# Three small edits to a fused retention and feed-forward kernel: the order of one down product, the slots of one block's attention steps, and the store of the last output

## The chip, the cores and the metric

One core of a Trainium2 chip. The metric is device time in microseconds (us), the median of several executions; ratios come with a 95% interval. A trace is one profiled execution of a kernel, timed from the start of its span.

## The reference, cut to what matters

```python
scores = scale * q @ k^T                      # 8 batches, 8 heads, 576 positions, 64 wide
ret = scores * (gamma_h ** (i - j) if i >= j else 0)
x = (ret @ v) regrouped to (4608 tokens, 512)
h = x @ w_in                                  # 512 -> 2048
g = h * clip(h + 3, 0, 6) / 6
out = g @ w_out                               # 2048 -> 512, float32
```

## The kernel before

The attention is done in chunks of 128 positions with a running state per head (each batch has four chunks of 128 and a rest of 64; they are numbered through all batches). The feed-forward part is done in token blocks: number 0 has 512 tokens, 1 to 3 are small, 4 to 10 have 512 each. I count blocks from 0, so "the first block" is number 0 and "the fourth block" is number 4. Pieces ("subs") of the feed-forward work, each worth one slot of about 0.87 us of TensorE (PE), are interleaved with attention steps by a list of slots that is written by hand. Each engine's own instructions stand in its queue in that order.

One attention step `i` asks every engine for something:

```python
    def step(i):
        stage(inter, i - 1)          # PE: state part of chunk i-1
        if chunks_at(i) < NCH:
            stage(update, i)         # PE: new state sum
            stage(keep, i)           # VectorE: state;  GpSimd: sd = state * decay
        stage(score, i)              # PE: scores;  VectorE: masked scores "at" (two)
        stage(mix, i - 1)            # PE: at @ v;  ScalarE: xt
        stage(cast, i + 3)           # GpSimd: three casts or products of loaded tiles
        if i + 3 > NCH + NPE - 1:
            stage(xpose, i + 3)      # SyncE: DMA transpose of q and k
        stage(load, i + 6)           # SyncE: loads
```

The first block's down product takes each 128-token row chunk `mc` through four quarters (`part`) of the second weight, which arrives by four DMAs, one per quarter:

```python
    def down(kb, mc, part):
        # ...
        for fc in range(m * part, m * part + m):
            nc.tensor.matmul(pout, gts[kb][:, fc, P * mc:P * mc + P],
                             wout16[:, fc, :],
                             start=(fc == 0), stop=(fc == NFC - 1))
        # part 3: copy to osb by ScalarE, give the PSUM bank back, store every second mc
```

From the fourth block on, the down product is a scheme of seven half-size products (`seven`), for each half `u` of the block, which needs four sums of activation quarters made by VectorE (`gsums`; eight instructions a block, two fp16 inputs from SBUF each):

```python
    def gsums(kb, i):
        # ...
        for u in range(2):
            nc.vector.tensor_tensor(out=s[i][:, :, u], in0=x[:, :, u],
                                    in1=y[:, :, u], op=op)
```

Order of a block: 16 up products (each followed by `u` on ScalarE and `gt` on VectorE), gsums 0 and 1, products 1 and 2 for both `u`, gsums 2 and 3, products 5 and 6, then 7, then 4 and 3. A block half's output is a tile `osb` of 128 x 2 x 512 floats, stored by one 512 KB DMA after product 3.

## Time and profile before

312.0 us (311.6 to 312.81, three runs). The page of the profiled run:

```profile
span 309.8 us, 6856 instructions
PE 295.2 (95%) x2644; PEld 190.1 (61%) x2644; DVE 234.5 (76%) x435; ACT 162.8 (53%) x307; POOL 125.8 (41%) x154
```

PE (TensorE) is busy for 295.2 us. What can be won without doing fewer matmuls is in the gaps. I cut the span by the starts of PE's first matmul of each stage in the timeline (the span is 309.77 us before the page rounds it):

| stretch of PE's time | us, before |
|---|---|
| start to the first block's first down matmul | 33.87 |
| from there to the second block's first up matmul | 17.94 |
| from there to the fourth block's first up matmul | 40.23 |
| from there to the next block's first up matmul | 35.24 |
| from there to the end of the last matmul | 178.35 |
| from there to the end of the span | 4.14 |

Here is PE's timeline in the first block's down product: start, duration, engine, line, output<-inputs, shapes, count, and in brackets the idle time just before and what ended it.

```profile
41.00 1.03 PE L529 MATMUL pout<-wout,gt 128*128 128x512 f16 x4
41.96 0.26 PE L327 MATMUL pm<-qkt 64*64 64x64 f16 x8
43.65 1.89 PE L529 MATMUL pout<-wout,gt 128*128 128x512 f16 x8 [1.43 <-DMA wout<-in_moe_w_out_dram]
```

Row chunk 0 has its quarter 2 at 41.00 and at once wants quarter 3, which lands 1.43 us too late.

The fourth block's seven products, on PE, VectorE (DVE) and GpSimd (POOL):

```profile
114.02 1.04 PE L594 MATMUL accz<-wt,gsum 128*128 128x256 f16 x8
116.91 1.05 PE L594 MATMUL accy<-wt,gsum 128*128 128x256 f16 x8 [1.85 <-DVE gsum L574]
120.83 1.05 PE L594 MATMUL accy<-wt,gsum 128*128 128x256 f16 x8 [0.25 <-DVE gsum L574]
...
110.82 0.85 DVE L305 TENSOR_TENSOR state<-pu,sd 64x256 f16<-64x256 f32 x2
111.70 1.29 DVE L333 TENSOR_TENSOR at<-pm,cmask 128x512 f16<-128x512 f32 x2
112.91 2.50 DVE L574 TENSOR_TENSOR gsum<-gt 128x1024 f16<-128x1024 f16 x2
115.33 2.54 DVE L574 TENSOR_TENSOR gsum<-gsum,gt 128x1024 f16<-128x1024 f16 x2
...
113.37 1.49 POOL L111 TENSOR_TENSOR natqk<-stgqk,wvq 128x512 f16<-128x512 f32 x1
114.82 1.49 POOL L114 TENSOR_TENSOR natv<-stgv,wvq 128x512 f16<-128x512 f32 x1
```

Two things delay the gsum that PE waits for. The step in slot 16 put 2.1 us of VectorE work (state and masked scores, 110.82 to 112.91) ahead of the gsums; and a pair of gsums takes 2.50 us here while GpSimd works beside them, and 1.29 in every later block, where it does not. GpSimd's products are slow at the same moment: 1.49 us against 1.04 elsewhere.

The end of the run:

```profile
304.59 1.04 PE L594 MATMUL accz<-wout,gsum 128*128 128x256 f16 x8
305.67 0.42 DVE L613 TENSOR_TENSOR osb<-accz,csum 128x256 f32<-128x256 f32 x1 [1.32 <-PE accz L594]
```

The last store (512 KB) is issued at 306.2, its bytes move until 308.3, and the span ends at 309.8. One of its windows of half a microsecond (start:end, length, busy time of PE, PEld, DVE, ACT, POOL with counts, granted clock, share of the 16 DMA engines, GB/s):

```profile
307.00:307.50 0.50, 0.00 (x0) 0.00 (x0) 0.00 (x0) 0.00 (x0) 0.00 (x0) 1.00 1.03 426
```

### The profile page before, as it was taken

Reading aid. Unit: us, or ns where it says so; the run is one execution under the profiler, and the core shown is the slowest. Engines: PE = TensorE matmul, PEld = TensorE weight load, DVE = VectorE, ACT = ScalarE, POOL = GpSimd, SP = SyncE. Lnnn points to the kernel's source line nnn. Section 1 sums busy time; section 2 is a strip of 40 time slices with the busy share of each in tenths; the row PEclk is TensorE's granted clock in tenths of the full one; section 3 lists DMA queues with packets and bytes.
Section 4 is the critical chain, followed back from the end, with each engine's and each line's share of the span. In section 5 each row is a group of like instructions: output and inputs, shape, how many; then the busy total and the mean of one; then the engine's idle time right before and its main releaser. Section 6 shows DMA issues by size and latency. Waiting matters only on the chain.

```text
span 309.8 us, 6856 instructions
## 1 busy us (share of the span) xinstructions
PE 295.2 (95%) x2644; PEld 190.1 (61%) x2644; DVE 234.5 (76%) x435; ACT 162.8 (53%) x307; POOL 125.8 (41%) x154
## 2 busy tenths in 40 slices
PE   7799989989999988999999999999999999999994
PEld 3454436677655467646864686468646864684583
DVE  6697447565948999699778977897789778856781
ACT  7567325565437732575357534753575347526721
POOL 3681139664576759052192409131754130000000
PEclk9999999999999999999999999999999999999998
DMA  7999999999799799999068965791694040003003
GB/s 247 204 194 196 196 193 209 238 240 220 174 202 246 177 220 235 187 252 203 9 155 234 215 146 135 223 236 40 187 245 111 2 156 0 2 0 138 1 0 138
DMA packets 143217, 49.61 MB, mean 160 GB/s; under 512 B 134224, under 2 KB 140368, under 8 KB 143184
## 3 DMA queue, kind: packets, MB, share of 16 engines
q1 hardware_dynamic: 138960, 44.97, 62.8%
q0 software_dynamic: 4224, 4.19, 8.2%
q8 instruction: 21, 0.34, 0.4%
q14 instruction: 12, 0.10, 0.1%
HBM read 36.70 MB, written 9.44 MB: 149 GB/s over the span
## 4 chain that ended last, share of the span: by engine, by line
PE 76%; DMA 10%; DVE 5%; POOL 3%; ACT 3%; issue 1%; SPq 0%; DVEq 0%
PE ph L512 35%; PE accy L594 15%; DMA wout<-in_moe_w_out_dram 7%; PE accz L594 7%; PE pout L529 6%; PE po L354 4%; PE accx L594 3%; PE pm L323 3%; DMA stgk<-in_k_dram 2%; DVE gsum L574 2%; PE po L252 2%; PE pu L274 2%; ACT u L516 1%; POOL natv L465 1%; DVE at L333 1%
## 5 line engine op out<-in xcount | busy, mean ns | idle before, releaser
L512 PE MATMUL ph<-xt,win 128*128 128x512 f16 (+2 forms) x704 | 130.1, 341 | 0.8 <-ACT xt L387 0.7
L517 DVE SCALAR_TENSOR_TENSOR gt<-u,ph 128x512 f16<-128x512 f32 x144 | 96.2, 686 | 29.4 <-ACT u L516 28.3
L516 ACT ACTIVATE u<-ph,cb 128x512 f32<-128x512 f32 x144 | 99.1, 688 | 35.1 <-PE ph L512 32.8
L512 PEld LDWEIGHTS <-win 128*128 128x128 f16 x704 | 61.6, 98 | 59.3 <-DMA win<-in_moe_w_in_dram 1.5
L310 POOL TENSOR_TENSOR sd<-state,gp 128x512 f32<-128x512 f16 x21 | 22.8, 1088 | 99.5 <-DVE state L305 62.1
L594 PEld LDWEIGHTS <-gsum 128*128 128x128 f16 x448 | 43.6, 98 | 7.8 <-DVE gsum L574 2.7
L604 ACT COPY csum<-accy 128x256 f32<-128x256 f32 x42 | 15.6, 373 | 46.3 <-PE accy L594 46.3
L387 ACT ACTIVATE xt<-po 128x512 f16<-128x512 f32 (+2 forms) x57 | 23.2, 438 | 30.2 <-PE po L354 29.8
L333 DVE TENSOR_TENSOR at<-pm,cmask 128x512 f16<-128x512 f32 x56 | 36.1, 687 | 0.9
L594 PEld LDWEIGHTS <-gt 128*128 128x128 f16 x336 | 31.8, 98 | 6.4 <-DVE gt L517 0.4
L111 POOL TENSOR_TENSOR natqk<-stgqk,wvq 128x512 f16<-128x512 f32 x28 | 30.5, 1091 | 6.0 <-DMA stgqk<-in_q_dram 6.0
L114 POOL TENSOR_TENSOR natv<-stgv,wvq 128x512 f16<-128x512 f32 x28 | 30.6, 1091 | 5.5 <-DMA stgv<-in_v_dram 5.5
L529 PE MATMUL pout<-wout,gt 128*128 128x512 f16 x128 | 30.7, 380 | 1.4 <-DMA wout<-in_moe_w_out_dram 1.4
L594 PE MATMUL accy<-wt,gsum 128*128 128x256 f16 x224 | 26.9, 273 | 2.1 <-DVE gsum L574 2.1
L110 POOL CAST natqk<-stgqk 128x512 f16<-128x512 f32 (+1 forms) x36 | 23.2, 645 | 6.0 <-PE ph L512 6.0
L305 DVE TENSOR_TENSOR state<-pu,sd 64x256 f16<-64x256 f32 x42 | 17.6, 420 | 5.4 <-PE pu L274 4.5
L574 DVE TENSOR_TENSOR gsum<-gt 128x1024 f16<-128x1024 f16 x28 | 20.3, 765 | 0.2
L529 PEld LDWEIGHTS <-gt 128*128 128x128 f16 x128 | 11.4, 98 | 13.7 <-issue 1.4
L354 PE MATMUL po<-at,natv 128*64 128x128 f16 (+1 forms) x320 | 15.8, 220 | 0.8 <-DVE at L333 0.7
L594 PE MATMUL accx<-wout,gt 128*128 128x256 f16 x112 | 14.9, 273 | 0.0
L594 PE MATMUL accy<-wt,gt 128*128 128x256 f16 x112 | 14.6, 273 | 0.0
L594 PE MATMUL accy<-wout,gt 128*128 128x256 f16 x112 | 14.5, 273 | 0.0
(75 smaller groups left out, 245.4 us busy)
## 6 DMA issues: line engine op xcount, KB each, us to landing
out_dram<-osb SPq DMA_DIRECT2D x17, 512.0 KB, 4.3
stgv<-in_v_dram SPq DMA_DIRECT2D x32, 256.0 KB, 4.3
stgqk<-in_k_dram SPq DMA_DIRECT2D x28, 256.0 KB, 3.7
stgqk<-in_q_dram SPq DMA_DIRECT2D x28, 256.0 KB, 4.0
win<-in_moe_w_in_dram POOLq DMA_DIRECT2D x4, 512.0 KB, 10.2
wout<-in_moe_w_out_dram POOLq DMA_DIRECT2D x4, 512.0 KB, 19.0
stgq<-in_q_dram SPq DMA_DIRECT2D x2, 512.0 KB, 5.3
stgk<-in_k_dram SPq DMA_DIRECT2D x2, 512.0 KB, 6.1
```

The costliest lines, as they stand in the source:

```text
L110: nc.gpsimd.tensor_copy(n16[:, 0], t[:, 0])
L111: nc.gpsimd.tensor_tensor(out=n16[:, 1], in0=t[:, 1], in1=w[:, 1].unsqueeze(2).to_broadcast(sh), op=ALU.mult)
L114: nc.gpsimd.tensor_tensor(out=v16, in0=tv, in1=w[:, 0].unsqueeze(2).to_broadcast(sh), op=ALU.mult)
L333: nc.vector.tensor_tensor(out=at, in0=pms[e], in1=w[:, e], op=ALU.mult)
L354: nc.tensor.matmul(o_ap, v_ap, a_ap, start=(c == 0 and pr == 0), stop=True, skip_group_check=True)
L387: nc.scalar.mul(x, src, inv_sqrt_d)
L512: nc.tensor.matmul(ph[:, j, :], win16[:, dmc, P * fc:P * fc + P], xts[kb][:, dmc, :], start=(dmc == 0), stop=(dmc == NCC - 1))
L516: nc.scalar.activation(u, ph, ACTF.Relu, bias=cb[:, 0:1], scale=1.0 / 6.0)
L517: nc.vector.scalar_tensor_tensor(out=gts[kb][:, g * m:g * m + m, :], in0=u, scalar=1.0, in1=ph, op0=ALU.min, op1=ALU.mult)
L529: nc.tensor.matmul(pout, gts[kb][:, fc, P * mc:P * mc + P], wout16[:, fc, :], start=(fc == 0), stop=(fc == NFC - 1))
L574: nc.vector.tensor_tensor(out=s[i][:, :, u], in0=x[:, :, u], in1=y[:, :, u], op=op)
L594: nc.tensor.matmul(o, a[:, f, u, :], w[:, f, :], start=(first and f == 0), stop=(f == HF - 1), skip_group_check=True)
```

## The change

Intent: (1) use all four row chunks' quarter-2 matmuls to cover the arrival of quarter 3; (2) move the attention steps of the fourth block so that they stay clear of its gsums; (3) leave only a quarter of the last tile to be stored after the last addition.

```diff
@@ seven(): the last block's second half
         elif p == 4:
             nc.scalar.copy(osb[:, 1, 0:HD], o)
             done_with(t)
+            if tok0 + 256 * u + 256 == NTOK:
+                o2 = out[NTOK - 256:NTOK, :].rearrange("(p h) n -> p h n", h=2)
+                nc.sync.dma_start(o2[:, 0, 0:HD], osb[:, 0, 0:HD])
+                nc.sync.dma_start(o2[:, 1, :], osb[:, 1, :])
@@ after product 3
-            nc.sync.dma_start(
-                out[tok0 + 256 * u:tok0 + 256 * u + 256, :].rearrange(
-                    "(p h) n -> p h n", h=2), osb)
+            o2 = out[...].rearrange("(p h) n -> p h n", h=2)
+            if tok0 + 256 * u + 256 == NTOK:
+                nc.sync.dma_start(o2[:, 0, HD:DM], osb[:, 0, HD:DM])
+            else:
+                nc.sync.dma_start(o2, osb)
@@ the order of the first block's down product
-            parts.sort(key=lambda x: (x[1] // 2, x[1] if x[1] < 2 else 0))
+            parts.sort(key=lambda x: x[1])
@@ the slots of the fourth block's six steps
-    due[NEAR:last[5] + 1] = [starts[4] + x for x in (0, 3, 7, 11, 16, 26)]
+    due[NEAR:last[5] + 1] = [starts[4] + x for x in (-0.5, 3, 8, 13, 24, 27)]
```

(`out[...]` stands for the same slice as in the removed lines.) The old order was quarters 0 and 1 for all four chunks, then quarters 2 and 3 chunk by chunk.

More of the change, by code (lines that the diff above doesn't have):

```diff
@@ L615, in seven @@
             done_with(t)
-            nc.sync.dma_start(
-                out[tok0 + 256 * u:tok0 + 256 * u + 256, :].rearrange(
-                    "(p h) n -> p h n", h=2), osb)
+            o2 = out[tok0 + 256 * u:tok0 + 256 * u + 256, :].rearrange(
+                "(p h) n -> p h n", h=2)
+            if tok0 + 256 * u + 256 == NTOK:
+                nc.sync.dma_start(o2[:, 0, HD:DM], osb[:, 0, HD:DM])
+            else:
+                nc.sync.dma_start(o2, osb)
         if p == 7:
```

## The prediction

> **What bounds the kernel now.** The page gives TensorE (PE) 295.2 us busy in a span of 309.8, at a granted clock of 0.997. The windows table (5 us stretches) shows PE full from 125 us to the end of its work at 305.6, so any microsecond PE gains earlier should reach the end one to one. PE's 14.6 us of idle time lie in four places: the start-up before 20 us (about 5, untouched), the first block's down product (1.43), the fourth block (2.6), and the tail after the last matmul (4.2).
>
> **1. First block, weight quarters outermost.** The timeline has PE idle 1.43 us at 42.2-43.65, waiting for the last weight-out quarter (the chain shows it landing at 43.6). Row chunk 0 asks for quarter 3 straight after quarter 2. In the new order the quarter-2 matmuls of all four chunks come first: 12 more matmuls at 0.216 us, 2.6 us, plus interleaved attention work, so quarter 3 is first needed near 45.6, two us after it lands. The wait should vanish. Cost: four PSUM banks are held longer, and four evictions (0.59 us each) and two stores bunch up; at most 0.2 us of waits. Saving 1.4 us.
>
> **2. Fourth block, step slots.** PE waits 0.53 us at 104.3 (a bank), 1.85 at 116.9 and 0.25 at 120.8 (gsum). The eight gsum additions of this block take about 1.25 us each (2.5 per pair); in the next block 0.64 (1.29 per pair). What differs is GpSimd: busy 5.00 of 5 us at 115-120 here, idle during the next block's gsums; its casts stretch from 1.04 to 1.49 us at the same moment. The Trainium skill, "SBUF — State Buffer", section "Who interferes with whom", says a VectorE instruction with two SBUF inputs contends with a GpSimd instruction that reads SBUF; this trace agrees. The step at slot 16 puts 2.1 us of VectorE work (state, masked scores) ahead of the gsums, and its state releases GpSimd's scaling and three chunks of casts right over them. Moved to slot 24, it follows the gsums in VectorE's queue, and GpSimd, in order, waits for that state. Then the gsums start about 2 us earlier and run at 0.64 us, as two blocks later, where the slots are nearly alike and PE never waits. Saving 2.5 us. Later casts should still meet their transposes with some 4 us to spare.
>
> **3. Tail.** The last 512 KB store is issued at 306.2; half-microsecond windows show its data moving at about 418 GB/s until 308.3, and the span ends 1.5 us later. Only 128 KB will now follow the last addition: 0.3-0.6 us of data instead of 1.25 (pieces are 1 KB instead of 4 KB); the fixed parts stay. Saving 0.8 us.
>
> **Sum.** 1.4 + 2.5 + 0.8 = 4.7 us, all on the critical path: 307.3 us, range 306.2 to 309.0. Chance of over 2% faster 0.05, within 2% 0.94, over 2% slower 0.01.
>
> **What would show it.** No DMA wait on the first down product; no gsum wait in the fourth block; all gsums near 0.69 us, no 1.5 us maximum; GpSimd idle during them; last matmul near 301.7; from it to the end about 3.4 us.
>
> **What would make it wrong.** GpSimd's casts still overlapping the gsums; the step at slot 24 or 27 meeting a VectorE backlog, so that PE waits for masked scores; delayed casts making transposes late; three small stores costing more to issue than they save.

## The result, and the profile after

307.55 us (306.47 to 308.54, five runs) against 311.62 (310.83 to 312.81, five runs): ratio 0.9859, interval 0.9822 to 0.9896. A ratio is the mean time of one kernel's runs over that of the other's of the same rounds, so not quite the ratio of the medians quoted. Executions over 1.5% slower than the fastest of the same kernel are left out of the means. The gain is under 2%, as the prediction had it.

```profile
span 305.7 us, 6860 instructions
PE 295.6 (97%) x2644; PEld 190.3 (62%) x2644; DVE 230.5 (75%) x435; ACT 162.5 (53%) x307; POOL 122.5 (40%) x154
```

The same cuts of PE's time, with a second trace of the same changed kernel (run e4 below):

| stretch | before | after | after again (e4) |
|---|---|---|---|
| start to the first down matmul | 33.87 | 33.06 | 32.86 |
| to the second block's first up | 17.94 | 16.46 | 16.45 |
| to the fourth block's first up | 40.23 | 40.21 | 40.21 |
| to the next block's first up | 35.24 | 33.87 | 32.52 |
| to the end of the last matmul | 178.35 | 178.35 | 178.33 |
| to the end of the span | 4.14 | 3.79 | 3.85 |
| sum | 309.77 | 305.74 | 304.22 |

The first row is not the change's work: nothing before the first down matmul was touched, and it moves by itself from run to run. The three edits gave, between these two traces, 1.48, 1.37 and 0.35 us. The 178 us after the fourth block are the same to 0.02 us, so what PE gains earlier does reach the end.

The first block's down product after, on PE:

```profile
40.20 1.03 PE L529 MATMUL pout<-wout,gt 128*128 128x512 f16 x4
41.15 0.26 PE L327 MATMUL pm<-qkt 64*64 64x64 f16 x8
41.34 1.90 PE L529 MATMUL pout<-wout,gt 128*128 128x512 f16 x8
...
43.49 1.04 PE L529 MATMUL pout<-wout,gt 128*128 128x512 f16 x4
44.36 0.61 PE L220 MATMUL pst<-ident,natqk 128*128 128x128 f16 x8
44.81 1.03 PE L529 MATMUL pout<-wout,gt 128*128 128x512 f16 x4
```

Quarter 2 now runs at 40.20, 41.34 and 43.49; the first matmul on quarter 3 is at 44.81, and no bracket stands anywhere. The fourth block after, again PE, VectorE, GpSimd:

```profile
111.56 1.04 PE L594 MATMUL accz<-wt,gsum 128*128 128x256 f16 x8
112.43 1.04 PE L594 MATMUL accy<-wt,gsum 128*128 128x256 f16 x8
113.31 1.04 PE L594 MATMUL accz<-wt,gsum 128*128 128x256 f16 x8
...
109.67 1.29 DVE L574 TENSOR_TENSOR gsum<-gt 128x1024 f16<-128x1024 f16 x2
110.88 1.28 DVE L574 TENSOR_TENSOR gsum<-gsum,gt 128x1024 f16<-128x1024 f16 x2
115.77 0.86 DVE L305 TENSOR_TENSOR state<-pu,sd 64x256 f16<-64x256 f32 x2 [0.54 <-PE pu L274]
...
116.77 1.04 POOL L310 TENSOR_TENSOR sd<-state,gp 128x512 f32<-128x512 f16 x1 [7.58 <-DVE state L305]
118.32 1.04 POOL L111 TENSOR_TENSOR natqk<-stgqk,wvq 128x512 f16<-128x512 f32 x1
```

The gsums are at full speed, GpSimd sits idle for 7.58 us over them because it waits, in order, for a state that is now made after them, and PE runs through. But PE has a wait in this block that it did not have before:

```profile
99.30 0.40 PE L323 MATMUL pm<-qkt 64*128 64x128 f16 x8 [1.27 <-DMA qkt<-natqk]
```

It is for a DMA transpose, at the step of slot 8. And the end of the run after:

```profile
300.91 1.04 PE L594 MATMUL accz<-wout,gsum 128*128 128x256 f16 x8
301.62 0.67 SPq L612 DMA_DIRECT2D out_dram<-osb  x1
301.98 0.42 DVE L618 TENSOR_TENSOR osb<-accz,csum 128x256 f32<-128x256 f32 x1 [1.32 <-PE accz L594]
302.43 0.36 SPq L624 DMA_DIRECT2D out_dram<-osb  x1
```

Windows of half a microsecond show the DMA engines at 346 to 434 GB/s from 301.5 to 304.0 without a gap; two of them:

```profile
302.50:303.00 0.50, 0.00 (x0) 0.00 (x0) 0.00 (x0) 0.00 (x0) 0.00 (x0) 1.00 0.91 346
303.00:303.50 0.50, 0.00 (x0) 0.00 (x0) 0.00 (x0) 0.00 (x0) 0.00 (x0) 1.00 1.13 420
```

### The profile page after: what moved, and what is told of

It reads as the page before. It is cut to its first block, busy times and chain, and to the rows that moved or that the text cites. A ratio compares the mean times of both kernels' runs of the same rounds, so it can differ in the third digit from the quotient of the medians.

```text
span 305.7 us, 6860 instructions
## 1 busy us (share of the span) xinstructions
PE 295.6 (97%) x2644; PEld 190.3 (62%) x2644; DVE 230.5 (75%) x435; ACT 162.5 (53%) x307; POOL 122.5 (40%) x154
## 4 chain that ended last, share of the span: by engine, by line
PE 85%; DMA 5%; DVE 4%; ACT 3%; issue 1%; POOL 1%; SPq 0%; DVEq 0%; POOLq 0%
PE ph L512 37%; PE accy L594 16%; PE accz L594 8%; PE pout L529 8%; PE accx L594 4%; PE po L354 4%; PE pm L323 3%; DMA stgq<-in_q_dram 2%; DMA qkt<-natqk 2%; PE po L252 2%; PE pu L274 2%; DVE at L333 1%; ACT u L516 1%; ACT qkt L222 1%; DVE gt L517 1%
## 5 line engine op out<-in xcount | busy, mean ns | idle before, releaser
L111 POOL TENSOR_TENSOR natqk<-stgqk,wvq 128x512 f16<-128x512 f32 x28 | 29.2, 1042 | 6.5 <-DMA stgqk<-in_q_dram 6.5
L110 POOL CAST natqk<-stgqk 128x512 f16<-128x512 f32 (+1 forms) x36 | 21.3, 591 | 6.9 <-DMA stgqk<-in_k_dram 6.9
L574 DVE TENSOR_TENSOR gsum<-gt 128x1024 f16<-128x1024 f16 x28 | 18.0, 685 | 0.2
L594 PE MATMUL accz<-wout,gsum 128*128 128x256 f16 x112 | 14.5, 273 | 0.0
```

The source lines that it names most:

```text
L110: nc.gpsimd.tensor_copy(n16[:, 0], t[:, 0])
L111: nc.gpsimd.tensor_tensor(out=n16[:, 1], in0=t[:, 1], in1=w[:, 1].unsqueeze(2).to_broadcast(sh), op=ALU.mult)
L594: nc.tensor.matmul(o, a[:, f, u, :], w[:, f, :], start=(first and f == 0), stop=(f == HF - 1), skip_group_check=True)
```

## The experiments

Eleven runs. The first table gathers them; "quarter wait" is PE's wait for the last weight-out quarter, "block" the time from the fourth block's first up matmul to the next block's, "transposes" PE's waits in that block which the trace puts down to a DMA transpose, "tail" the time from the last matmul's end to the span's end.

| run | ratio (interval) | quarter wait | block | transposes | tail |
|---|---|---|---|---|---|
| before | | 1.43 | 35.24 | (0.53) | 4.14 |
| after | 0.9859 (0.9822 to 0.9896) | 0 | 33.87 | 1.27 | 3.79 |
| e1_down | 0.9999 (0.9947 to 1.0052) | 0 | 34.88 | 0.16 | 4.15 |
| e2_slots | 0.9898 (0.9854 to 0.9942) | 0.80 | 32.52 | 0 | 4.13 |
| e3_tail | 0.9989 (0.9940 to 1.0038) | 0 | 34.93 | 0.22 | 5.21 |
| e4_after | 0.9864 (0.9820 to 0.9907) | 0 | 32.52 | 0.20 | 3.85 |
| e5_before_held | 0.9937 (0.9887 to 0.9986) | 1.44 | 36.52 | 4.12 | 4.13 |
| e6_after_early | 0.9830 (0.9779 to 0.9881) | 0 | 34.34 | 0.71 (1.14) | 3.79 |
| e7_parts | 0.9819 (0.9775 to 0.9862) | 0 | 34.65 | 2.28 | 3.51 |
| e8_late_pe | one look | 0.28 | 35.19 | 0.48 | 4.15 |
| e9_pool_reads | one look | 0 | 37.01 | 1.91 | 3.80 |
| e10_pool_writes | one look | 0 | 32.53 | 0 | 3.79 |
| e11_no_down | 0.9937 (0.9884 to 0.9991) | 1.65 | 32.52 | 0 | 3.80 |

e1 to e4 shared one chip, e5 to e8 another, e9 to e11 a third; the median of the kernel before was 310.78, 313.9 and 310.54 us on them. (The two figures in brackets are put down to a ScalarE and a VectorE instruction by the table of waits, but PE's weight loads for the same matmuls waited 0.70 and 1.31 us for a DMA transpose.)

### The three parts alone, and the whole again (e1, e2, e3, e4)

Edits: e1 is the kernel before with only the new `parts.sort`, e2 with only the new slots, e3 with only the new stores; e4 is the changed kernel again.

> The first part alone (quarters outermost in the first block's down product). Theory: the 1.43 us wait for the last weight-out quarter goes and PE stays earlier by about 1.45 us up to the fourth block; there some of it may be given back, because the transposes of the first steps of that block do not come earlier with PE (in the changed kernel's trace PE waited 1.27 us for one). Theory says 0.9950 to 0.9985 of before in time (0.5 to 1.5 us), the wait for the weight quarter absent, and any loss visible as a PE wait for a transpose. Rival: the wait only moves to another place in the first three small blocks (banks, evictions bunched): then PE reaches the fourth block at the same time as before and the ratio is 1.000.

> The second part alone (step slots of the fourth block). Theory: the three waits of that block (2.63 us) go, the gsums run at 0.64 us each, ratio 0.990 to 0.993 (2.2 to 3.0 us); as PE is not earlier at the block's start than in the kernel before, the wait of 1.27 us for a transpose is absent or under 0.5 us. Rival: the transpose wait is made by the new slots themselves and also stands here; then the gain is about 1.4 us, ratio 0.9955.

> The third part alone (last output in three parts). Theory from the changed kernel's trace: the last megabyte of stores is moved without a gap at some 420 GB/s from the moment the last but one 512 KB store is issued, so the end is set by that stream and not by the last 128 KB: from the start of the last addition to the end 3.7 us instead of 4.1, gain 0.4 us, ratio 0.9987. My prediction said 0.8 us, ratio 0.9974, and 3.4 us.

> The whole change again, for the sum beside its parts on one chip: ratio 0.986 (4.4 us). If the transpose wait of 1.27 us in its first trace was one bad moment of the DMA queues (bytes moved fell to nearly nothing for 2 us), it is absent or much smaller in this trace; if it belongs to the new order, it stands again at about 1 us. Parts that do not interact would add up: the sum of the three gains equals this one; if the first part's gain is lost on transposes, the sum is larger by up to 1.3 us.

Measured. **e2**: the slots alone gave a ratio of 0.9898; the block fell to 32.52 us, all three of its waits gone. The rival, that the new slots make a transpose wait, fell. **e4**: the ratio repeated (0.9864), and the transpose wait was 0.20 us, not 1.27. **e1**: in the trace the quarter wait is gone and the distance from first down matmul to second block is 16.44 us, as in the changed kernel, and nothing is given back in the small blocks (40.22 us) and little on transposes (0.16). But the time did not move: 0.9999, with an interval of half a per cent, 1.6 us, to either side. In this trace the gain was not lost later; the measured times could not show a gain of this size. **e3**: the ratio agrees with 0.4 us as well as with 0; this trace's tail was 5.21 us, and after 308.0 a small rest (8 to 23 GB/s in the windows) trickled until 309.5. All other kernels with the same stores have 3.79 to 3.85, so I leave this one out. The three ratios together give 1.1% and the whole gives 1.4%; the intervals do not tell those apart.

e3 shows why the first part's gain is hard to see. It has the old down order and no quarter wait at all:

```profile
42.67 1.03 PE L529 MATMUL pout<-wout,gt 128*128 128x512 f16 x4
43.63 0.26 PE L327 MATMUL pm<-qkt 64*64 64x64 f16 x8
43.82 1.90 PE L529 MATMUL pout<-wout,gt 128*128 128x512 f16 x8
```

Its start-up was late (first up matmul at 21.73 us, against 19.80 in the trace of before and 18.80 to 19.31 in the others without added work), so PE came to quarter 3 after it had landed, and from the first down matmul to the second block it took 16.45 us, as with the new order.

### Does the quarter land when it lands, whatever PE does? (e8, e11)

```diff
+    idle(10)          # e8, in the kernel before: ten useless matmuls ahead of the first up matmul
     load_win(3)
```

e11 is the changed kernel with the old `parts.sort`.

> The kernel before with ten idle matmuls (2.16 us, of which 0.69 fill an existing wait) ahead of the first up-matmul: PE comes about 1.5 us later to the first block. Theory (the last weight-out quarter lands at a time set by GpSimd's issue and the DMA queues, 41.9 to 43.6 us in six traces, whatever PE does): the wait for it falls to zero or by 1.5 us, and the second block starts at 51.4 to 52.2 us, as in the kernel before; so the first part of the change is worth only what PE's early start leaves. Rival (the landing slides with PE): the wait stays 0.7 to 1.4 us and everything is 1.5 us later.

> The changed kernel with the first part undone (the first block's down product as before). Theory: PE waits for the last weight-out quarter again, by 0 to 1.4 us depending on how early the start-up of that run was (its first up-matmul at 19.1 us gives 0.7 to 1.4, later than 21 us gives none), and nothing else changes: slots' gain stands, ratio 0.988 to 0.992. Rival (the first part hurt or helped elsewhere, by banks or bunched evictions in the small blocks): the distance from the first block's down product to the second block, less this wait, differs from 16.45 us by more than 0.2.

In e8 the quarter landed at 43.2 us (issued at 20.5, 22.7 to land), PE came at 43.0, and the wait shrank to 0.28:

```profile
43.30 1.89 PE L529 MATMUL pout<-wout,gt 128*128 128x512 f16 x8 [0.28 <-DMA wout<-in_moe_w_out_dram]
```

The second block started at 51.46, inside what the theory gave and earlier than in the kernel before (51.81) although 2.16 us of work had been added. In this one trace the landing does not follow PE; in all thirteen it came between 41.5 and 43.6 us. In e11 the wait is back:

```profile
42.91 1.89 PE L529 MATMUL pout<-wout,gt 128*128 128x512 f16 x8 [1.65 <-DMA wout<-in_moe_w_out_dram]
```

It is 1.65 us, a little over the expected range, at a first up matmul of 19.09 us. First down matmul to second block is 18.15 us, less the wait 16.50: the order costs and gains nothing else. Its ratio, 0.9937, is smaller a gain than expected, though its interval holds the 0.9898 of e2, which has the same block and the same down order. So the first part removes a wait of 0.80 to 1.65 us when the start-up is early (four traces of the old order), and removes nothing when it is late (e3, one trace).

### What made the gsums late: GpSimd beside them, or the work ahead of them in VectorE's queue? (e5, e6, e9, e10)

e5 keeps the old slots, and with them the 2.1 us of step work ahead of the gsums; only GpSimd is held off until the gsums are done:

```diff
+    def held_casts(kb):               # called after gsums 2 and 3 of the fourth block
+        g = work.tile([P, 4], FP16, tag="gate", bufs=1, name="gate")
+        nc.gpsimd.tensor_copy(g[:, 0:1], st["g", kb][3][:, HF - 1, 1, P - 1:P])
+        for i in (17, 18):
+            cast_ahead(i)             # cast and xpose of step i, taken out of step(i)
```

> The kernel before, slots untouched; only GpSimd is kept off the fourth block's gsums: its casts of steps 17 and 18 wait, behind a one-element copy of the last gsum, until the gsums are done. The step of slot 16 still stands ahead of the gsums on VectorE. Theory (the gsums are slow because GpSimd reads SBUF beside them): gsums of this block near 0.64 us each instead of 1.25, GpSimd casts 1.04 instead of 1.49, PE's gsum waits of 2.1 us fall to at most 0.3 although VectorE starts them as late as before (2.1 us after the last gt); block from first up-matmul to the next block's first 32.7 to 33.2 us instead of 35.2. Rival (the 2.1 us of step work ahead in VectorE's queue makes the wait): gsums may be faster or not, but PE still waits about 1.5 us or more at the first sum of the second kind.

```profile
114.56 1.29 DVE L333 TENSOR_TENSOR at<-pm,cmask 128x512 f16<-128x512 f32 x2
115.77 1.28 DVE L587 TENSOR_TENSOR gsum<-gt 128x1024 f16<-128x1024 f16 x2
...
121.39 0.19 POOL L502 COPY gate<-gsum 128x1 f16<-128x1 f16 x1 [5.68 <-DVE gsum L587]
...
116.88 1.04 PE L607 MATMUL accz<-wt,gsum 128*128 128x256 f16 x8
117.75 1.04 PE L607 MATMUL accy<-wt,gsum 128*128 128x256 f16 x8
```

The gsums begin 2.40 us after the first of the seven products (113.37), exactly as late as in the kernel before (110.51 and 112.91). Still PE waits for none of them. From the first of the seven products to the next block's first up matmul it took 14.32 us, against 16.77 in the kernel before: 2.45 us. So the queue order alone costs PE nothing, and the waits went with the contention alone. The block as a whole did not reach the 33 us expected, for another reason: PE waited 4.12 us for three DMA transposes at 95, 101 and 107 us, all before the point where this edit begins; less these it is 32.40 us. The ratio was 0.9937 all the same.

e6 was meant as the reverse: the new slots, with two chunks' casts let go early.

> The changed kernel, slots as changed; only GpSimd's casts of two chunks are let go before the state of the step at slot 24, so that they run over the gsums again. VectorE's order is that of the changed kernel. Theory (contention): gsums 1.25 us each while GpSimd runs, about six of the eight; PE waits about 0.9 us for a gsum and up to 1.5 us later for masked scores; block 33.4 to 35 us instead of 32.5. Rival (queue order alone): gsum waits stay absent, block 32.5 us (plus at most 0.3 for a transpose).

It failed as a test. The loads of those chunks came only after the first two sums (GpSimd waited 2.63 us for one), so the casts ran over the third and fourth. Pairs of those took 2.13 us, but PE has slack there and waited for none of them (15.63 us for the seven-product stretch). It shows the slow gsums again and says nothing about PE. Its block of 34.34 us lies in the range that the contention theory gave, but by luck: PE waited 1.85 us for transposes at the block's first steps.

e9 and e10 put useless GpSimd work over the gsums of the changed kernel, started by the block's last `gt`:

```diff
+        nc.gpsimd.tensor_copy(g[:, 0:1], gts[kb][:, NFC - 1, 511:512])
+        for i in range(5):            # e9: reads two SBUF tiles
+            nc.gpsimd.tensor_tensor(out=d, in0=cmask[...], in1=cmask[...], op=ALU.mult)
+        for i in range(12):           # e10 instead: only writes
+            nc.gpsimd.memset(d, float(i))
```

> The changed kernel with useless work on GpSimd laid over the fourth block's gsums: five products of two SBUF tiles (128x512, 1.04 us each alone), started by the block's last gt. VectorE's order is untouched; nothing that VectorE or PE need comes later than the end of that work. Theory (a GpSimd instruction that reads SBUF slows a VectorE addition with two SBUF inputs): the gsums it covers take about 1.2 us from start to start instead of 0.6, GpSimd's products 1.5 us instead of 1.04, and PE waits about 0.9 us for the first sum of the second kind, perhaps 1 to 1.5 us more for masked scores; from the first product of seven to the next block's first up-matmul 16.5 to 18 us instead of 15.6 to 15.9. Rival (the slots alone matter): gsums 0.64, 15.6 to 15.9 us.

> As the run before it, but GpSimd's useless work is twelve fills of a 128x512 tile, which only write SBUF. If reading is what contends, as the Trainium skill has it, the gsums stay at 0.64 us and PE waits for none (15.6 to 15.9 us). If any GpSimd work on SBUF slows them, they show 1.2 us as beside the products.

First e9 (VectorE, GpSimd, PE), then e10 (VectorE, GpSimd):

```profile
111.31 3.43 DVE L574 TENSOR_TENSOR gsum<-gsum,gt 128x1024 f16<-128x1024 f16 x2
115.33 2.77 DVE L574 TENSOR_TENSOR gsum<-gt 128x1024 f16<-128x1024 f16 x2
...
110.80 8.43 POOL L583 TENSOR_TENSOR idlew<-cmask 128x512 f16<-128x512 f32 x5
...
121.21 0.40 PE L252 MATMUL po<-qkt,state 128*128 128x128 f16 x4 [1.13 <-DVE state L305]
```

```profile
109.59 1.29 DVE L574 TENSOR_TENSOR gsum<-gsum,gt 128x1024 f16<-128x1024 f16 x2
...
109.05 6.92 POOL L583 MEMSET idlew<- 128x512 f16 x12
```

With reads, pairs of gsums took up to 3.43 us, the five products 8.43 us, and the seven-product stretch 18.23 us, a little more than I had allowed (this product was never run alone; the casts' products take 1.04 us each alone). The gsum wait of 0.9 us that I expected did not come. Most of PE's loss came not at a gsum but after them, as waits of 1.13 and 0.42 us for VectorE's state and masked scores, which stood behind the slow gsums in its queue; the rest is spread over the gsum products, of which sixteen matmuls took 2.24 us instead of 1.92. With writes only, the gsums kept their 1.29 a pair, PE waited for nothing and the stretch took 15.86 us, as in the changed kernel. The Trainium skill, "SBUF — State Buffer", section "Who interferes with whom", says that a VectorE instruction with two SBUF inputs contends with a GpSimd instruction that reads SBUF, and not with one that only writes it. These two runs agree with both halves.

### What bounds the tail? (e7)

```diff
+    def store_part(kb, u, osb, h, n0):          # last block only, both halves u
+        t0 = blocks[kb][0] + 256 * u
+        o2 = out[t0:t0 + 256, :].rearrange("(p h) n -> p h n", h=2)
+        nc.sync.dma_start(o2[:, h, n0:n0 + HD], osb[:, h, n0:n0 + HD])
     # called after products 2, 7, 4 and 3, each as soon as its quarter of osb is complete
```

> The changed kernel, with both halves of the last block's output stored in parts, each as soon as it is done, so that 768 KB of the last megabyte leave before the last additions. Theory (the changed tail is bound by one stream of stores from the last but one store on): from the last matmul's end to the end of the run 3.1 to 3.3 us instead of 3.75 to 3.83, that is what the prediction said of the change itself. Rival (fixed costs of issue and completion after the last addition bound it, or the many small stores are slower): 3.7 us or more.

The tail was 3.51 us: about 0.3 better than the changed kernel's, but not the 3.1 to 3.3 expected. Both views hold a part. Half of the last megabyte left early, and the last 128 KB took 1.9 us from issue to landing, where they took 2.4 in the changed kernel. But the span ended 1.2 us after that landing instead of 0.9, which took half of it back; why is not shown. And the small stores moved more slowly than the large ones had. Windows of half a microsecond of e7:

```profile
302.50:303.00 0.50, 0.48 (x5) 0.18 (x2) 0.00 (x0) 0.01 (x1) 0.00 (x0) 1.00 0.75 262
303.00:303.50 0.50, 0.00 (x0) 0.00 (x0) 0.42 (x1) 0.00 (x0) 0.00 (x0) 1.00 0.20 72
303.50:304.00 0.50, 0.00 (x0) 0.00 (x0) 0.00 (x0) 0.00 (x0) 0.00 (x0) 1.00 0.55 191
```

No window of its stores passes 266 GB/s, where the 4 KB pieces of the kernel before went at 401 to 426. That is mostly the gaps between stores that become ready one after the other, since the DMA engines were busy for 17 to 76% of these windows. The 1 KB pieces are the smaller part: from 303.4 to 303.6 us, with the 16 engines busy for 99%, they moved at 353 GB/s, against 410 for 4 KB pieces in the kernel before. Its time (0.9819) is the lowest ratio measured, but it was taken on another chip than the changed kernel's, on which e6, with the stores of the changed kernel, had 0.9830. That it is faster than the changed kernel rests on 0.3 us in the trace and is not shown by the measured times.

## Why the prediction was right

The time (307.3 predicted, 307.55 measured) and the direction were right. That they agree to 0.25 us is luck: the five runs spread over 2.1 us. The terms, one by one:

1. **First part, 1.4 us predicted.** The mechanism is right: the wait is gone in all seven traces with the new order, and nothing else changed. Between the two first traces it was 1.48. But I took the size from one trace as if it were fixed. Over the traces with the old order it was 1.43, 0.80, 0, 1.44 and 1.65 (e8, with work added, apart), because the quarter lands at its own time and PE's arrival hangs on the start-up.
2. **Second part, 2.5 us predicted.** e2, e4, e10 and e11 have a block of 32.52 or 32.53 us, 2.72 less than before, against 34.88 to 35.24 with the old slots and no disturbance: 2.4 to 2.7. The cause given was two-fold, work ahead in VectorE's queue and contention. e5 shows that the contention suffices and that the work ahead costs PE nothing without it. What the prediction called a bank wait (0.53 us) was most likely a wait for a DMA transpose, as PE's weight load shows it.
3. **What the prediction did not have.** It feared late transposes because of late casts; those casts were in time (no wait in the fifth block). PE waited instead at the fourth block's first steps, 1.27 us in the first trace after. In that trace the DMA engines moved 20 and 12 GB/s for two microseconds (windows 96 to 98 us) where they had moved 198 to 280 in the three before. Such falls are in every trace: between 30 and 130 us each of the thirteen has at least one window of 1 us under 50 GB/s, at varying times. The wait does not come with every run of the new order (the second trace has 0.20, e10 none), and the old slots in e5 have 4.12. But the change's part in it is not ruled out. Up to these steps after, e4, e6, e7, e9 and e10 are the same program with all three edits, and four of the six waited 1.27 to 2.28 us; of the other seven only e5 waited more than 0.53. So an earlier PE may meet late transposes more often and give back some of the first edit's gain. What stops the queues stays open.
4. **Tail, 0.8 us predicted, about 0.3 measured** (4.13 to 4.15 us with the old stores, 3.79 to 3.85 with the new, e3 and e7 apart). The failing step is "only 128 KB will now follow the last addition; the fixed parts stay". 128 KB follow it, but they queue behind the 512 KB store of the other half, issued only at 300.72, and behind 384 KB of their own tile. The whole megabyte moved as one stream from 301.5 to 304.1, so the rate of the queue set the end and not the size of the last piece. From issue to landing the last store took 2.6 us before and 2.4 after, though it is a quarter of the size; e7's last 128 KB, with less ahead of them, took 1.9.

So the sum of the first trace came out near 4 us because terms moved in opposite ways: the start-up gave 0.8 us by chance, the transpose wait took 1.3, and the tail gave less than half of what was predicted.

## What to carry to other kernels

When the same instruction takes twice as long in one stage as in another, look at what the other engines do beside it before reading the wait as a matter of order: here GpSimd work that read SBUF doubled the time of VectorE's additions, and one dependence that held GpSimd back (e5) removed the same waits as the rescheduling. A wait on a load is the difference of two times that vary from run to run, so one trace gives a sample of it and not its size. A last store that is cut small gains only until the stores ahead of it become the stream that ends last.

## What the Trainium skill lacked or had wrong

- "SBUF — State Buffer", "Who interferes with whom": right on reads against writes (e9, e10). It calls the shared ports an exclusive lock, by which one gsum and one product should take the sum of their times. From start to start a gsum alone takes 0.60 us and a casts' product alone 1.00, together 1.60. In e9, with products of two whole tiles, a gsum came every 1.68 us, near that sum. In the kernel before, where the product's second input is a small tile read again and again, a gsum beside one came every 1.45 us, less than the sum, so there the lock was not held for the whole of both.
- "DMA: Bandwidth & Descriptors", "Specifications", asks for at least 512 B a piece for line rate. Here pieces of twice that size were still slower: with the DMA engines fully busy, 1 KB pieces moved at 353 GB/s (e7) and 4 KB pieces at 410 (the kernel before).
- The same page has nothing on standstills of the DMA queues as seen here: 20 and 12 GB/s in the two microseconds from 96 us of the first trace after, 198 to 280 in the three before them.
- "TensorE: Matmul & The Clock Gate", "Part 1", puts the fall to half clock after an idle window of about 3.4 us. In e3 the granted clock was 1.00 up to 11 us and 0.50 from 12 to 14 us, after a PE gap of only 1.75 us: in the 3.41 us before the fall (7.87 to 11.28 us) PE was still busy for 1.38 us. In the kernel before, with 2.01 us busy from 7.43 to 10.84, the clock stayed at 1.00. So a window that is mostly idle was enough here. Eight transposing matmuls took 1.06 us at the lower clock and 0.62 before it, which added to that run's late start.
